# Filling TensorE's planned waits with products of ones, and planning the order for the full clock

## The chip, the cores and the metric

The kernel runs on one core of a Trainium2 chip. The metric is the device time of one execution in microseconds, lower is better. The core has five engines with a queue of their own each, which run in order and wait for one another by semaphores: TensorE (PE in the profile; its weight loads are PEld), VectorE (DVE), ScalarE (ACT), GpSimd (POOL) and SyncE (SP), which issues the transfers here.

## The reference

Two things follow one another. The first is attention with a mask: each query and each key of a head is assigned to the nearest of 16 centroids, and a query sees only the keys of its own cluster. The second is a feed-forward layer over the 3072 rows of the result.

```python
q_assign = np.argmax(np.einsum('bhsd,hcd->bhsc', q_n, c_n), axis=-1)
k_assign = np.argmax(np.einsum('bhsd,hcd->bhsc', k_n, c_n), axis=-1)
mask = q_assign[:, :, :, None] == k_assign[:, :, None, :]
scores = np.where(mask, scale * np.matmul(q, k.transpose(0, 1, 3, 2)), -1e9)
attn = softmax(scores)                    # 4 batches, 8 heads, 768 x 768, head size 64
x = np.matmul(attn, v)                    # as 3072 x 512
h = x @ w_in                              # 512 x 2048
g = np.where(h >= 1, h, np.where(h <= -1, 0.0, (h + 1) ** 2 / 4))
out = g @ w_out                           # 2048 x 512
```

## The kernel before

**The work.** Float32 operands are split into a high and a low float16 part, and each product is made of three products of parts. A pair of heads fills the 128 partitions, so there are 4 pairs in each of 4 batches. The queries are taken in chunks of 256 rows: 3 chunks a batch, 12 in all. For each chunk and head pair there are four score steps (`at_scores`, `at_soft`): products of queries and keys and of the cluster masks into a PSUM bank, a scaling with the row minimum on VectorE (the custom instruction that writes `sS`), the exponential on ScalarE, a split into high and low (`hl`) on ScalarE and GpSimd, and a transpose into `pT`, by the DMA engines or, in the early steps, by TensorE for every other step (the products `idf,sS`). Then `at_av` multiplies the transposed weights by the values into `bank_a`; ScalarE copies one part of it (`rb`) and VectorE multiplies the other by it. The result `x` of four head pairs is one input chunk of the feed-forward part (`ffn1`, `ffn2`).

**The start.** Ahead of the first scores the head pairs' k, q and v are loaded, scaled (`kv_scale`, with a small product of ones that spreads a maximum over the partitions, `am`), split and transposed (products `idf,n`), and assigned to centroids (products `cT,kvq`, then a series of small VectorE instructions). The feed-forward weights are loaded in 16 pieces and prepared during the first part of the run: absolute values on ScalarE, bit operations on VectorE (`wk`, `w`), column sums as products with ones (`wk,ones`), a scale, and a split on ScalarE and GpSimd.

**The order.** Nothing is issued directly. The code records every operation with its engine, its operands and a cost (`price`, in ns); `issue` then plans. `forward` runs the recorded operations through a model of the engines, the PSUM banks and the DMA queue, and takes on each engine the ready operation with the best due time; `backward` computes due times from the end. Eight rounds are made, and the order of the round with the shortest modelled span is issued, each engine in that order. In this model a TensorE operation that starts before `COLD` (75e3 ns) costs twice as much, since TensorE is expected to be at half clock there:

```python
clock[e] = t + x.cost * (2 if e == "tensor" and t < COLD else 1)
```

All instructions are issued from the last lines of `issue` (line 291 in the profile), so lines don't tell them apart there; the tiles' names do. `bank` are the three wide PSUM tiles, `banka` and `bankh` the two single banks. `bank_a` is used by `at_av` alone. `ones` is a 128x128 bfloat16 constant.

Of the kernel before, what the change touches and what calls it, by code (L numbers as in the profile page):

```python
# [27 lines left out]


LATENCY = dict(tensor=280, scalar=252, vector=230, gpsimd=175)  # L30
COLD, AHEAD = 75e3, 1500

LOOK, MARGIN = 0.4, 4000
ROUNDS = 8
# [3 lines left out]
class Recorder:  # L38
# [114 lines left out]
    def forward(self, prio):  # L153

        clock, ready, avail = {}, {}, {}
        left = {x: len(x.preds) for x in self.nodes}
        at = dict.fromkeys(self.nodes, 0.0)
        for x in self.nodes:
            if not x.preds:
                heappush(ready.setdefault(x.eng, []), (0.0, prio[x], x.i))  # L160
        hw, ring, sent, span = 450.0, 0.0, [], 0.0
        self.order, bank = [], {}
        todo = len(self.nodes)
        while todo:
            todo -= 1
            best = None
            for e, q in ready.items():
                now = clock.get(e, 0.0)
                a = avail.setdefault(e, [])
                while q and q[0][0] <= now:  # L170
                    _, s, i = heappop(q)
                    heappush(a, (s, i))
                t = now if a else q[0][0] if q else None
                if t is not None and (best is None or t < best[0]):
                    best = t, e
            t, e = best
            q = ready[e]
            while q and q[0][0] <= t:
                _, s, i = heappop(q)
                heappush(avail[e], (s, i))  # L180
            pick = heappop(avail[e])
            x = self.nodes[pick[1]]

            more = [(s, r, i) for r, s, i in q[:8] if r < t + x.cost * LOOK and s < pick[0] - MARGIN]
            if more:
                heappush(avail[e], pick)
                _, t, i = min(more)
                q.remove((t, prio[self.nodes[i]], i))
                heapify(q)
                x = self.nodes[i]  # L190

            free = max((until for k in x.banks for o, until in bank.get(k, {}).items() if o != e), default=0.0)
            if free > t:
                clock[e] = t
                heappush(q, (free, prio[x], x.i))
                todo += 1
                continue
            if x.dma and x.dma[0] > 256 and ring > t + AHEAD:

                clock[e] = t  # L200
                heappush(q, (ring - AHEAD, prio[x], x.i))
                todo += 1
                continue
            if x.dma:
                kb, tr = x.dma
                t = max(t, hw, sent[-8] if len(sent) > 7 else 0.0)
                clock[e] = t + x.cost
                hw = t + (650 if tr else 475)
                ring = max(ring, hw + (650 if tr else 784)) + kb * (5.6 if tr else 3.25)
                if tr:  # L210

                    hw = max(hw, ring - 1000)
                end = ring + (400 if tr else 1300)
                sent.append(end)
            else:
                clock[e] = t + x.cost * (2 if e == "tensor" and t < COLD else 1)
                end = clock[e] + LATENCY[e]
            for k in x.banks:
                bank.setdefault(k, {})[e] = end
            x.start, x.busy = t, clock[e]  # L220
            span = max(span, end)
            self.order.append(x)
            for y in x.succs:
                raw = x.dma or x.eng != y.eng or (y.preds[x] and x.eng != "tensor")
                at[y] = max(at[y], end if raw else x.busy)
                left[y] -= 1
                if not left[y]:
                    heappush(ready.setdefault(y.eng, []), (at[y], prio[y], y.i))
        return span
# [43 lines left out]
                    heappush(ready.setdefault("sync" if p.dma else p.eng, []), (at[p], -prio[p], -p.i))  # L273
        return start

    def issue(self):
        for x in self.nodes:
            for y in x.preds:
                y.succs.append(x)
        prio = {x: x.step for x in self.nodes}  # L280
        best = None
        for _ in range(ROUNDS):
            span = self.forward(prio)
            if best is None or span < best[0]:
                best = span, self.order
            prio = self.backward({x: x.start for x in self.nodes})
        span, self.order = best
        with self.tc.manual_schedule():
            for x in self.order:
                for fn, args, kw in x.calls:  # L290
                    fn(*args, **kw)  # L291

# [57 lines left out]
def tile_clustered_attention_moe(  # L350
# [10 lines left out]
    nc = tc.nc  # L361
# [6 lines left out]
    P = 128  # L368
# [21 lines left out]
    rec = Recorder(tc)  # L390
# [35 lines left out]
    bank = [psum.tile([P, 1024], F32, name=f"bank{i}") for i in range(3)]  # L426
    bank_a, bank_h = [psum.tile([P, 512], F32, name=f"bank{x}") for x in "ah"]
# [3 lines left out]
    start = iter([0, 1] * 2).__next__  # L431
# [28 lines left out]
    ones = const.tile([P, P], BF16, name="ones")  # L460
# [628 lines left out]
    for s in sorted(ev):  # L1089
        rec.step = s  # L1090
        for fn, args in ev[s]:
            fn(*args)
    rec.issue()


# [30 lines left out]
```

## Time and profile before

| | |
|---|---|
| three runs | 919.07, 917.01, 918.56 us (median 918.56) |
| the profiled execution | 917.96 us, its span on the engines 916.2 us |
| mean granted TensorE clock | 0.961 |
| busy, share of the span | PE 89%, PEld 62%, DVE 68%, ACT 72%, POOL 63% |
| TensorE in 0 to 23, 23 to 46, 46 to 69, 69 to 92 us | 5.71, 13.21, 12.37, 14.54 us busy |
| TensorE's waits up to 90 us, by the engine waited for | VectorE's `bank` 15.1 us in 6 waits, ScalarE's `sS` 11.8 in 5, ScalarE's `n` 6.5 in 1, VectorE's `n` 6.0 in 2 |

A row of the timeline has the start in us, the duration of a group in us, the engine, the line, the operation with output and inputs, the number of instructions, and in brackets the idle time ahead of it with the engine that ended it. The granted clock is a share of full speed as the profiler recorded it. A group's row has the busy time in us, the mean duration of one in ns, and the idle time ahead; matmuls overlap, so busy time over count is less than the mean of one.

### The profile page before, as it was taken

The page shows a single profiled execution, that of the slowest core. Times are in us where ns is not written, and L with a number is a line of the kernel's source. Part 1 is how long each engine was busy: PE and PEld are TensorE (multiplying, and loading weights), DVE is VectorE, ACT ScalarE, POOL GpSimd, SP SyncE. Part 2 cuts the span into 40 slices and gives each one's busy share as a digit, 9 for nine tenths or more (in the row PEclk, how much of TensorE's full clock was granted, in tenths as well). Part 3 has the DMA queues.
Part 4 walks back from the last instruction along what each step waited for, and adds up shares of the span by engine and source line. Part 5 has one row for each costly group of instructions (what it writes and reads, how often), then busy time and mean ns, then how long its engine had stood idle before and what let it go on. Part 6 is the DMA issues. An engine that isn't in the chain of part 4 may idle for free.

```text
span 916.2 us, 19559 instructions
## 1 busy us (share of the span) xinstructions
PE 819.7 (89%) x7462; PEld 566.2 (62%) x7462; DVE 621.8 (68%) x1335; ACT 660.5 (72%) x1145; POOL 580.4 (63%) x521
## 2 busy tenths in 40 slices
PE   2556669899998999999998999999998999999998
PEld 2344446556765766776666666666665666667664
DVE  6999987887796665556987665557868555444232
ACT  5778999979767587778676687678766677776232
POOL 1369888986764667766575677656565666666322
PEclk9756779999999999999999999999999999999999
DMA  9989675658998878868899968878998866666100
GB/s 312 238 204 189 133 208 129 152 120 183 185 201 166 161 141 164 156 147 187 166 205 167 176 124 163 157 155 195 178 196 149 149 132 127 111 121 110 30 24 24
DMA packets 403263, 142.82 MB, mean 156 GB/s; under 512 B 380000, under 2 KB 395360, under 8 KB 403168
## 3 DMA queue, kind: packets, MB, share of 16 engines
q1 hardware_dynamic: 403168, 141.56, 76.3%
q8 instruction: 58, 0.95, 0.4%
q14 instruction: 37, 0.30, 0.1%
HBM read 40.40 MB, written 6.29 MB: 51 GB/s over the span
## 4 chain that ended last, share of the span: by engine, by line
PE 68%; DVE 14%; issue 4%; ACT 2%; POOL 2%; ACTq 0%; DVEq 0%; POOLq 0%
PE bank L291 51%; PE banka L291 10%; PE bankh L291 8%; DVE sS L291 3%; DVE r L291 2%; DVE bank L291 2%; DVE kvq L291 2%; DVE n L291 1%; POOL hl L291 1%; DVE w L291 1%; ACT sS L291 1%; DVE mx L291 1%; ACT hl L291 0%; ACT wk L291 0%; DVE bankh L291 0%
## 5 line engine op out<-in xcount | busy, mean ns | idle before, releaser
L291 POOL TENSOR_TENSOR hl<-sS,hl 128x768 f16<-128x768 f32 x181 | 311.4, 1723 | 138.2 <-ACT hl L291 122.1
L291 PE MATMUL bank<-w,g 128*128 128x512 f16 x1152 | 272.7, 380 | 3.0 <-ACT o L291 1.8
L291 PEld LDWEIGHTS <-w 128*128 128x128 f16 x2304 | 223.8, 98 | 62.4 <-issue 21.7
L291 DVE CUSTOM_DVE_ANT_0 sS<-bank,zero,er 128x768 f32<-128x768 f32 x192 | 194.2, 1012 | 88.6 <-PE bank L291 68.2
L291 PEld LDWEIGHTS <-kvq 128*128 128x128 f16 (+1 forms) x3264 | 191.3, 107 | 88.8 <-issue 43.2
L291 ACT ACTIVATE sS<-sS,sbi 128x768 f32<-128x768 f32 x192 | 179.3, 934 | 87.0 <-DVE sbi L291 83.3
L291 PEld LDWEIGHTS <-g 128*128 128x128 f16 x1152 | 111.1, 98 | 120.6 <-POOL g L291 3.3
L291 PE MATMUL bank<-kvq 128*128 128x384 f16 x768 | 163.1, 337 | 17.4 <-DVE sbi L291 7.7
L291 POOL TENSOR_TENSOR g<-r,g 128x512 f16<-128x512 f32 x88 | 104.5, 1187 | 87.3 <-ACT g L291 87.2
L291 ACT CAST hl<-sS 128x768 f16<-128x768 f32 x181 | 148.8, 825 | 3.1 <-DMA pT<-hl 1.7
L291 PE MATMUL bank<-x,w 128*128 128x256 f16 x1056 | 127.9, 274 | 7.2 <-DVE bank L291 3.5
L291 ACT ACTIVATE r<-r,f_ra,f_rs 128x512 f32<-128x512 f32 x88 | 71.3, 810 | 59.0 <-DVE r L291 58.6
L291 PE MATMUL banka<-pT,kvq 128*64 128x256 f16 x1728 | 105.9, 278 | 0.0
L291 DVE TENSOR_SCALAR r<-bank,f_lo,f_hi 128x512 f32<-128x512 f32 x60 | 48.5, 808 | 39.6 <-PE bank L291 32.7
L291 ACT CAST g<-r 128x512 f16<-128x512 f32 x88 | 53.8, 611 | 22.4 <-DVE r L291 13.9
L291 PE MATMUL bank<-wk,w 128*128 128x256 f16 x504 | 60.2, 273 | 4.0 <-DVE bank L291 1.9
L291 POOL TENSOR_TENSOR w<-w 128x1024 f32<-128x1024 f32 (+1 forms) x24 | 52.1, 2177 | 10.6 <-ACT w L291 10.6
L291 PE MATMUL bankh<-x,w 128*128 128x256 f16 x480 | 57.0, 273 | 1.6 <-DVE r L291 1.5
L291 DVE SCALAR_TENSOR_TENSOR r<-bank,f_gs,r 128x512 f32<-128x512 f32 x60 | 44.8, 746 | 13.3 <-ACT r L291 11.3
L291 POOL TENSOR_TENSOR n<-n,phi 128x768 f16<-128x768 f16 x14 | 21.6, 1540 | 28.9 <-DMA kvq<-n 14.9
L291 ACT ACTIVATION_READ_ACCUMULATOR sS<-sS,sbi 128x1 f32 x192 | 36.0, 187 | 0.0
L291 DVE TENSOR_SCALAR r<-bankh,f_lo,f_hi 128x512 f32<-128x512 f32 x28 | 22.6, 809 | 19.5 <-PE bankh L291 16.7
(180 smaller groups left out, 884.0 us busy)
## 6 DMA issues: line engine op xcount, KB each, us to landing
w<-in_moe_w_out_dram SPq DMA_DIRECT2D x14, 512.0 KB, 4.4
kvq<-in_k_dram SPq DMA_DIRECT2D x16, 384.0 KB, 3.8
kvq<-in_q_dram SPq DMA_DIRECT2D x16, 384.0 KB, 3.9
kvq<-in_v_dram SPq DMA_DIRECT2D x16, 384.0 KB, 4.2
out_dram<-o SPq DMA_DIRECT2D x11, 512.0 KB, 3.8
w<-in_moe_w_in_dram SPq DMA_DIRECT2D x10, 512.0 KB, 5.3
n<-in_moe_w_in_dram SPq DMA_DIRECT2D x6, 512.0 KB, 4.2
o<-in_v_dram SPq DMA_DIRECT2D x8, 384.0 KB, 3.9
```

Source lines behind the costliest of these rows:

```text
L291: fn(*args, **kw)
```

## The change

Two things change, and both act through the order.

`COLD` goes from 75e3 to 15e3: the model doubles TensorE's costs only up to 15 us. The eight rounds are made again with that, so the whole order of all five engines is a new one, with the same operations.

While issuing, the planned start and end of every operation is now known. Ahead of each TensorE operation that is planned to start before 300 us (`WARM`), and that starts over 600 ns (`PAUSE`) after the end of the one before it, products are put in: each multiplies the constant `ones` by four repetitions of itself (512 columns) into `bank_a`, at 217 ns (`FILL`) of the planned wait each, as many as fit, from a planned 10 us on. Nobody reads them. None is put in while a result in `bank_a` is planned to be still unread, and not before the last reader's planned end and latency.

```diff
-COLD, AHEAD = 75e3, 1500
+COLD, AHEAD = 15e3, 1500
+
+
+WARM, PAUSE, FILL = (10e3, 300e3), 600, 217
...
-            self.order.append(x)
+            self.order.append((x, t, x.busy))
...
-    def issue(self):
+    def issue(self, idle, bank):
...
-            for x in self.order:
+            done, free, unread = 0.0, 0.0, set()
+            for x, start, busy in self.order:
+                own = any(name == bank for name, _ in x.banks)
+                if x.eng == "tensor":
+                    t = max(done, free, WARM[0])
+                    while not unread and start < WARM[1] and t + FILL < start and start - done > PAUSE:
+                        idle()
+                        t += FILL
+                    done = busy
+                    if own:
+                        unread = {y for y in x.succs if y.eng != "tensor" and any(name == bank for name, _ in y.banks)}
+                elif own:
+                    unread.discard(x)
+                    free = max(free, busy + LATENCY[x.eng])
                 for fn, args, kw in x.calls:
                     fn(*args, **kw)
...
-    rec.issue()
+    still = ones.unsqueeze(1).to_broadcast([P, 4, P])
+    rec.issue(lambda: nc.tensor.matmul(bank_a, ones, still, start=True, stop=True), bank_a.tensor.name)
```

In the new kernel the products of ones have line 1111, everything else that the planner issues has line 308. The order holds 194 products of ones, each with a weight load. Three places follow.

TensorE at about 17 us, between the maximum of the values (`v_am`) and the scale of the third head pair (`am_132`), before:

```order
L291 MATMUL bank_76<-v_am_130,ones 128x4
L291 LDWEIGHTS ones
L291 MATMUL bank_76<-am_133,ones 128x2
L291 LDWEIGHTS ones
L291 MATMUL bank_75<-wk_66,ones 128x128
...
L291 MATMUL bank_76<-am_132,ones 128x2
L291 LDWEIGHTS n_72
L291 MATMUL bank_74<-idf,n_72 128x128
```

The same place now:

```order
L308 MATMUL bank_76<-v_am_130,ones 128x4
L1111 LDWEIGHTS ones
L1111 MATMUL banka<-ones 128x512
...
L308 MATMUL bank_76<-am_133,ones 128x2
L1111 LDWEIGHTS ones
...
L1111 MATMUL banka<-ones 128x512
L308 LDWEIGHTS ones
L308 MATMUL bank_76<-am_132,ones 128x2
L308 LDWEIGHTS ones
L308 MATMUL bankh<-n_72,ones 128x32
```

Two products of ones stand ahead of `am_133` and sixteen ahead of `am_132`; the eight column sums of the first weights (`wk_66`) have moved to a later place, and the mask sums (`bankh<-n_72,ones`) stand ahead of the transposes (`idf,n_72`).

TensorE at about 60 us, ahead of the third of the transposes of softmax weights (`idf,sS_81`), before:

```order
L291 MATMUL bank_75<-kvq_62 128x384
L291 LDWEIGHTS kvq_62
L291 MATMUL bank_75<-kvq_62 128x384
L291 MATMUL bank_74<-idf,sS_81 128x128 x6
```

The same place now:

```order
L308 MATMUL bank_75<-kvq_62 128x384
L308 LDWEIGHTS kvq_62
L308 MATMUL bank_75<-kvq_62 128x384
L1111 LDWEIGHTS ones
L1111 MATMUL banka<-ones 128x512
...
L1111 MATMUL banka<-ones 128x512
L308 MATMUL bank_74<-idf,sS_81 128x128 x6
```

Twenty-two products of ones stand between the scores (`kvq_62`) and these transposes.

VectorE from the first score step on (`sS` with its minimum `sbi`), before:

```order
L291 ISA sS_80,sbi_156<-bank_74,zero,er_148 128x768
L291 ISA sbi_156 128x1
L291 TENSOR_SCALAR bank_76<-bank_76 128x2
L291 TENSOR_SCALAR wk_66<-wk_66 128x1024
L291 TENSOR_SCALAR bank_76<-bank_76 128x1
L291 ISA sS_81,sbi_157<-bank_75,zero,er_148 128x768
```

The same place now, with the third and second score steps far behind the first:

```order
L308 TENSOR_SCALAR wk_66<-wk_66 128x1024
L308 TENSOR_REDUCE mx_146<-bank_76 128x24
L308 ISA sS_80,sbi_156<-bank_74,zero,er_148 128x768
L308 ISA sbi_156 128x1
L308 TENSOR_SCALAR w_iw_0_119<-bank_75 128x1
...
L308 ISA sS_79,sbi_158<-bank_74,zero,er_148 128x768
...
L308 SCALAR_TENSOR_TENSOR w_73<-w_73,wk_66 128x1024
...
L308 ISA sS_81,sbi_157<-bank_75,zero,er_148 128x768
```

The second score step (`sbi_157`) followed the first after three other instructions; now it stands behind the third (`sbi_158`), and a step of the weights' bit operations (`wk_66`, `w_73`) has moved ahead of each. Across all engines the planned operations are the same as before; the run of ones on TensorE is what is added.

## The prediction

> **What bounds the kernel now.** I read the page first, then the stretches (busy time by engine), then who waits for whom, and last TensorE's instructions in order of time.
>
> ```profile
> span 916.2 us, 19559 instructions
> PE 819.7 (89%) x7462; PEld 566.2 (62%) x7462; DVE 621.8 (68%) x1335; ACT 660.5 (72%) x1145; POOL 580.4 (63%) x521
> 10.00:35.00 25.00, 12.37 (x148) 9.67 (x149) 22.63 (x50) 16.45 (x25) 4.92 (x5) 1.00 0.98 313
> 35.00:92.00 57.00, 33.30 (x333) 24.62 (x332) 55.94 (x108) 44.96 (x59) 42.03 (x27) 0.58 0.92 199
> 92.00:138.00 46.00, 29.00 (x230) 19.97 (x229) 40.53 (x94) 44.11 (x68) 39.70 (x30) 0.78 0.66 169
> 138.00:184.00 46.00, 40.30 (x367) 28.12 (x365) 36.27 (x106) 43.00 (x72) 41.20 (x33) 0.96 0.62 141
> 184.00:916.00 732.00, 704.60 (x6394) 483.67 (x6391) 463.15 (x965) 505.98 (x912) 450.63 (x405) 1.00 0.76 146
> ```
>
> In a stretch's row the columns are its length, then busy us (with instructions) of PE, PEld, DVE, ACT, POOL, then granted clock, DMA share and GB/s. From 184 us on TensorE works 704.60 of 732 us at the full clock: there it is the bound. Before that another engine is full in each stretch: VectorE (55.94 of 57 us up to 92), then ScalarE (44.11 of 46 and 43.00 of 46). TensorE is idle in two fifths of 35 to 138 us, and its clock is 0.58 and 0.78. So a faster TensorE helps in the first part only where the full engine waits for it.
>
> The clock row needs a correction. It says 1.00 up to 35 us, but the same work takes there as long as in the half-clock part:
>
> ```profile
> 28.55 2.72 PE L291 MATMUL bank<-kvq 128*128 128x384 f16 x8 [1.54 <-ACT kvq L291]
> 91.48 1.46 PE L291 MATMUL bank<-kvq 128*128 128x384 f16 x8 [0.30 <-DVE pT L291]
> 19.77 1.01 PE L291 MATMUL bank<-wk,ones 128*128 128x128 bf16 x8 [0.43 <-DVE wk L291]
> 92.78 0.62 PE L291 MATMUL bank<-wk,ones 128*128 128x128 bf16 x8
> ```
>
> Eight score products take 2.72 us at 28.55 and 1.46 at 91.48, eight weight-sum products 1.01 and 0.62. The ratio is 1.86 and 1.63; so TensorE is slow from its first product on.
>
> **The products of ones.** The order holds 194 of them, in 26 runs: 156 ahead of the first attention-times-values group, 28 in four runs up to the first hidden layer's products, and 10 far back in TensorE's full part. The nearest row for one is the other 128x512 product:
>
> ```profile
> L291 PE MATMUL bank<-w,g 128*128 128x512 f16 x1152 | 272.7, 380 | 3.0 <-ACT o L291 1.8
> 17.16 0.17 PE L291 MATMUL bank<-v_am,ones 128*128 128x4 bf16 x1
> 23.33 0.19 PE L291 MATMUL bank<-am,ones 128*128 128x2 bf16 x1 [2.55 <-DVE bank L291]
> 61.81 1.54 PE L291 MATMUL bank<-idf,sS 128*128 128x128 f32 x6 [5.77 <-ACT sS L291]
> ```
>
> That is 272.7 / 1152 = 0.237 us each, and by the ratio 1.86 about 0.44 us at half clock. All 194 are 46 us at the full clock. From 10 to 138 us TensorE is idle 25 + 57 + 46 - 12.37 - 33.30 - 29.00 = 53.3 us now. A mean clock of 0.58 means half clock for 0.84 of the time, 0.78 for 0.44; a full clock would leave 33.30 x 0.42 + 29.00 x 0.22 = 20 us more idle. So they fit in total; they cost nothing where the wait behind them is really there. The run of 22 ahead of the transposes of sS is 22 x 0.237 = 5.2 us in a wait that is 5.77 us now: covered by ScalarE's exponential. The 16 + 2 between v_am and the second am are the worst case, since the clock is still low there: 18 x 0.44 = 7.9 us, in a gap of 23.33 - 17.16 = 6.2 us. The product behind them can be 1.7 us late, and less if the clock rises under way. What covers this is VectorE's queue, full for 22.63 of 25 us: 0 to +1.7 us; I take 0, since 24 transposes stand behind it and gain from the same clock.
>
> **What the faster clock gives.** Who waits for TensorE up to 92 us, and the pieces of the chain that ended last that are TensorE's from 100 to 126 us:
>
> ```profile
> DVE w_am L291 <- PE bank L291: 0.5, 1, 0.5
> DVE kvq L291 <- PE bank L291: 0.4, 1, 0.4
> DVE sS L291 <- PE bank L291: 0.4, 1, 0.4
> DVE sc L291 <- PE bank L291: 0.3, 1, 0.3
> DVE bank L291 <- PE bank L291: 0.2, 1, 0.2
> ...
> 103.16 3.68 PE bank L291 x18
> 106.83 2.31 PE banka L291 x44
> 109.14 0.77 PE bank L291 x4
> 119.54 1.54 PE bank L291 x6
> 121.08 3.66 PE banka L291 x35
> ```
>
> (a) 23 to 92 us. VectorE, the full engine, waits 0.5 + 0.4 + 0.4 + 0.3 + 0.2 = 1.8 us for TensorE. Half the time of the work waited for is the slow clock: -0.9 us. VectorE's own next instruction is late next.
>
> (b) 92 to 138 us. The same groups stand in the timeline slow and fast:
>
> ```profile
> 103.16 1.54 PE L291 MATMUL bank<-idf,sS 128*128 128x128 f32 x6 [3.26 <-ACT sS L291]
> 104.49 1.06 PE L291 MATMUL bank<-wk,ones 128*128 128x128 bf16 x8
> 105.35 1.49 PE L291 MATMUL bank<-kvq 128*128 128x384 f16 x4
> 107.01 2.13 PE L291 MATMUL banka<-pT,kvq 128*64 128x256 f16 x36
> 112.19 0.87 PE L291 MATMUL bank<-idf,sS 128*128 128x128 f32 x6 [1.19 <-ACT sS L291]
> 121.44 3.30 PE L291 MATMUL banka<-pT,kvq 128*64 128x256 f16 x36
> 129.11 0.81 PE L291 MATMUL bank<-kvq 128*128 128x384 f16 x4
> ```
>
> Transposes 1.54 against 0.87, twice; weight sums 1.06 against 0.62; scores 1.49 against 0.81; attention times values 3.30 against 2.13: 1.34 + 0.44 + 0.68 + 1.17 = 3.6 us on the chain. ScalarE is late next: its idle time in the stretch is 46 - 44.11 = 1.9 us, so -1.9 is all it can give.
>
> How far the clock holds here is open. From the run ahead of the first attention-times-values group to the one ahead of the third, over 206 products of the kernel's own, the new order has no product of ones.
>
> ```profile
> 90.00:93.00 3.00, 2.70 (x34) 2.00 (x31) 3.00 (x6) 2.97 (x4) 3.00 (x2) 1.00 1.32 142
> 93.00:96.00 3.00, 1.27 (x13) 0.92 (x11) 2.97 (x14) 2.60 (x6) 3.00 (x2) 1.00 0.97 163
> 96.00:99.00 3.00, 2.53 (x14) 1.51 (x14) 2.69 (x6) 3.00 (x6) 1.91 (x4) 0.59 0.92 337
> 94.81 0.87 PE L291 MATMUL bank<-idf,sS 128*128 128x128 f32 x6 [1.42 <-ACT sS L291]
> ```
>
> At 93 to 96 us TensorE works 1.27 of 3 us, its longest wait is 1.42 us, and right after it the clock is 0.59. So waits of that length let it fall, and I count (b) at the capped -1.9, not at 3.6. The Trainium skill ("TensorE: Matmul & The Clock Gate", section "Why this matters for your kernels") says that gaps between bursts may last up to about 3 us before the clock goes back; this trace disagrees, with 1.42 us as the longest wait ahead of the fall. By that rule the clock would stay up through the unfilled stretch; this is a rival below.
>
> (c) 138 to 184 us. The clock is 0.96, so half-clock time is 0.04 x 46 / 0.5 = 3.7 us; TensorE is busy 88% and loses 3.7 x 0.5 x 0.88 = 1.6 us. The order has 23 products of ones just ahead of this stretch and none in it, so I take a third: -0.5 us.
>
> (d) The new order itself. VectorE and ScalarE hold the same instructions; the last weight instruction of either stands behind the same 36 and 37 score steps as before. Some early weight steps stand ahead of scores that they followed. Nothing prices this: 0, with bounds from the idle time of the full engines from 10 us on, (25 - 22.63) + (57 - 55.94) + 1.9 + (46 - 43.00) = 8.3 us as the most that a better order and clock together can gain, and the rival below as the loss.
>
> **Sum.** -0.9 - 1.9 - 0.5 = -3.3 us on the profiled execution's 917.96, 914.7. That execution is 0.6 us under the median of 918.56; on the median the forecast is 915.3 us. About 0.2% (1.8 us) is what a measurement of this kernel can tell from no change.
>
> **Rivals.**
>
> No change, 918.6 us. The products run, but VectorE and ScalarE set the pace, and their waits for others take the place of the 1.8 and 1.9 us. For it: the full one of the two is above 95% busy from 35 to 138 us. Against it: the chain does pass through TensorE for 12 us there. The same time comes out if the products run at half clock and never lift it. Chance 0.22.
>
> Slower, 922.7 us. TensorE takes its queue in order, so where the wait is shorter than the order's own costs assume, the real product stands behind products of ones. The five longest runs are 16, 14, 18, 17 and 22, 87 products, 20.6 us; if their waits are a fifth shorter than planned, 4.1 us reach VectorE, which is full there. It decides once VectorE's waits for TensorE from 23 to 92 us grow from 1.8 to over 6 us. For it: the runs fill the whole expected wait without a margin, and the first run is planned at half its price. Against it: the 5.77 us wait above holds its run. The Trainium skill (same page, section "Part 2: What happens when you issue a matmul") says that matmuls stay in program order, which would make each late product late in full. Chance 0.25.
>
> The clock holds throughout, 913.3 us. Then (b) gives its 3.6 us, if the new order takes from ScalarE's queue what now stands ahead of those steps, and (c) half of its 1.6: 918.56 - 0.9 - 3.6 - 0.8 = 913.3. The Trainium skill's rule on gaps, above, would have it so. Against it stands the fall after 1.42 us. Chance 0.11.
>
> **The numbers.** The forecast has 0.42. Faster by over 0.2% is the forecast and the last rival, 0.53; within it 0.22; slower 0.25. The range goes up to the slower rival, 922.7, and down to the gain of 8.3 us with 1.8 us for a luckier order in the full part (27.4 us idle from 184 on): 908.5. Cases of both signs matter, so the forecast's own range: 912.5 to 916.7.
>
> **What would show it.** Right: a clock of 0.9 or more from 25 to 80 us, score groups of eight near 1.5 us, VectorE's waits for TensorE under 1 us up to 92, TensorE 95% busy from about 180 us on. Wrong: the clock still near 0.5 in 35 to 92; or real products that start later behind products of ones than their operands; or a gain or loss that arises behind 184 us, which would be the order's and not the clock's.

## The result, and the profile after

The change made the kernel slower: 928.97 us (median of 5 runs, 926.85 to 930.18) against 918.56 us (917.01 to 919.15), a ratio of 1.0114 with a 95% interval of 1.0095 to 1.0133. The forecast was 915.3 us, and its range ended at 922.7.

The profiled execution of the changed kernel took 928.97 us. Its page, to be laid beside the one in the prediction:

```profile
span 927.2 us, 19941 instructions
PE 856.3 (92%) x7656; PEld 578.0 (62%) x7656; DVE 623.8 (67%) x1335; ACT 659.9 (71%) x1145; POOL 573.0 (62%) x521
```

Its stretches (length, then busy us of PE, PEld, DVE, ACT, POOL, then granted clock, DMA share, GB/s):

```profile
10.00:35.00 25.00, 22.85 (x226) 13.69 (x227) 21.06 (x46) 14.78 (x23) 4.70 (x5) 0.93 0.96 309
35.00:92.00 57.00, 46.20 (x386) 27.15 (x384) 55.72 (x116) 47.11 (x64) 40.37 (x25) 0.88 0.89 216
92.00:138.00 46.00, 31.56 (x250) 20.83 (x249) 39.03 (x90) 39.52 (x60) 37.97 (x30) 0.80 0.62 146
138.00:184.00 46.00, 40.86 (x346) 28.11 (x345) 37.01 (x93) 42.19 (x69) 38.75 (x30) 0.98 0.52 121
184.00:916.00 732.00, 706.31 (x6419) 484.90 (x6419) 466.01 (x977) 506.77 (x917) 447.31 (x409) 1.00 0.77 147
```

The products of ones did what they are for: from 35 to 92 us the clock is 0.88 instead of 0.58. VectorE is as full there as before (55.72 of 57 us). From 92 to 138 us the clock gained only 0.02, and ScalarE, which was full with 44.11 us, now works 39.52: taken as a whole, nobody is full in this stretch any more (VectorE still is from 92 to 104 us, with 12.00 of 12 us), and the engines wait for one another.

What TensorE does at the place of its longest new wait, in order of time (start, duration, idle time ahead in brackets):

```profile
100.66 1.46 PE L308 MATMUL bank<-kvq 128*128 128x384 f16 x8 [1.55 <-DVE pT L308]
107.16 1.01 PE L308 MATMUL bank<-wk,ones 128*128 128x128 bf16 x8 [5.04 <-DVE sbi L308]
...
128.88 2.13 PE L308 MATMUL banka<-pT,kvq 128*64 128x256 f16 x36
```

And VectorE there:

```profile
97.08 2.66 DVE L308 SCALAR_TENSOR_TENSOR n<-n,wk 128x1024 uint32<-128x1024 uint32 x1
102.34 2.76 DVE L308 SCALAR_TENSOR_TENSOR w<-w,wk 128x1024 uint32<-128x1024 uint32 x1
105.02 1.00 DVE L308 CUSTOM_DVE_ANT_0 sS<-bank,zero,er 128x768 f32<-128x768 f32 x1
106.11 0.98 DVE L308 CUSTOM_DVE_ANT_0 sS<-bank,zero,er 128x768 f32<-128x768 f32 x1
```

TensorE has the scores done at 102.1 us and then stands still for 5.04 us: its next product needs the bank that a score step reads. On VectorE one of the weights' bit operations, of 2.66 us, has just ended then (97.08); another one, of 2.76 us, stands ahead of that score step (102.34), and two score steps of 1.0 us each run before the bank is free. This wait was made by the order, not by the products of ones: it is there without them too, as the first experiment shows.

From 184 to 525 us, in the part where TensorE is the bound, two groups of its waits for VectorE (us, times, longest) and the stretch, before (two fences) and now (two more):

```profile
PE bank L291 <- DVE bank L291: 2.8, 5, 1.2
PE bank L291 <- DVE sbi L291: 1.8, 3, 0.9
```

```profile
184.00:525.00 341.00, 326.12 (x3065) 224.32 (x3063) 245.45 (x530) 249.39 (x453) 224.35 (x199) 1.00 0.87 168
```

```profile
PE bank L308 <- DVE sbi L308: 6.8, 9, 1.6
...
PE bank L308 <- DVE bank L308: 5.1, 4, 3.0
```

```profile
184.00:525.00 341.00, 322.16 (x3026) 220.90 (x3027) 243.29 (x532) 244.82 (x446) 218.12 (x199) 0.99 0.87 165
```

The waits for a bank that a score step reads (`sbi`) went from 1.8 to 6.8 us. TensorE works 4.0 us less in the same 341 us, and 2.4 us of what it does work are the last ten products of ones (at 0.237 us).

Where the time went can be followed by the attention-times-values groups of 36 products, 48 in all, counted in order of time. The first of them, and VectorE's second score step of the order before (`sbi_157`), before (first two lines) and now:

```profile
34.45 1.00 DVE L291 CUSTOM_DVE_ANT_0 sS<-bank,zero,er 128x768 f32<-128x768 f32 x1
65.88 3.76 PE L291 MATMUL banka<-pT,kvq 128*64 128x256 f16 x36
47.53 1.01 DVE L308 CUSTOM_DVE_ANT_0 sS<-bank,zero,er 128x768 f32<-128x768 f32 x1
72.45 2.13 PE L308 MATMUL banka<-pT,kvq 128*64 128x256 f16 x36
```

The loss arises in two places. The first group already starts 6.6 us late, so most of the early loss is there before the 5.04 us wait; the fourth starts 7.4 us late (121.44 us before, 128.88 now, the last row of TensorE's above). The score step that was moved behind the weight steps runs 13 us later, but no run separates which of the moves makes the first group late. Most of that is caught up: the 14th group is 1.3 us late (315.88 and 317.20). Then the time is lost again, far behind the part that the change is about: the 26th group is 9.6 us late (515.43 and 525.06), and the last one 11.0 us (856.86 and 867.88).

### The profile page after: what moved, and what is told of

Read it like the earlier page. It is cut to its first block, busy times and chain, and to the rows that moved or that the text cites. A ratio compares the mean times of both kernels' runs of the same rounds, so it can differ in the third digit from the quotient of the medians.

```text
span 927.2 us, 19941 instructions
## 1 busy us (share of the span) xinstructions
PE 856.3 (92%) x7656; PEld 578.0 (62%) x7656; DVE 623.8 (67%) x1335; ACT 659.9 (71%) x1145; POOL 573.0 (62%) x521
## 4 chain that ended last, share of the span: by engine, by line
PE 65%; DVE 11%; issue 3%; ACT 3%; POOL 1%; ACTq 0%; DVEq 0%; POOLq 0%
PE bank L308 49%; PE banka L308 8%; PE bankh L308 8%; DVE r L308 2%; DVE sS L308 2%; DVE bank L308 2%; DVE kvq L308 1%; DVE n L308 1%; ACT sS L308 1%; POOL g L308 1%; DVE mx L308 1%; ACT n L308 1%; ACT hl L308 0%; ACT g L308 0%; POOL hl L308 0%
## 5 line engine op out<-in xcount | busy, mean ns | idle before, releaser
L308 POOL TENSOR_TENSOR hl<-sS,hl 128x768 f16<-128x768 f32 x181 | 306.1, 1695 | 137.1 <-ACT hl L308 120.4
L308 PEld LDWEIGHTS <-kvq 128*128 128x128 f16 (+1 forms) x3264 | 187.9, 105 | 86.4 <-issue 41.5
L308 PE MATMUL bank<-kvq 128*128 128x384 f16 x768 | 158.7, 330 | 18.9 <-DVE sbi L308 10.3
L1111 PE MATMUL banka<-ones 128*128 128x512 bf16 x194 | 52.3, 417 | 2.7 <-DVE rb L308 2.7
L1111 PEld LDWEIGHTS <-ones 128*128 128x128 bf16 x194 | 19.6, 106 | 30.8 <-issue 16.0
```

The source lines that it names most:

```text
L1111: rec.issue(lambda: nc.tensor.matmul(bank_a, ones, still, start=True, stop=True), bank_a.tensor.name)
```

## The experiments

Two theories stood at the start. O: the new order costs the time. F: the products of ones cost it, by standing ahead of real products. Ratios are to runs of the kernel before on the same chip (918.0 to 918.4 us).

**The order alone.** The changed kernel without any product of ones; the order of everything else is the same.

```diff
-WARM, PAUSE, FILL = (10e3, 300e3), 600, 217
+WARM, PAUSE, FILL = (10e3, 0.0), 600, 217
```

> The new order (planned with COLD at 15e3) without any product of ones; the kernel's own work is unchanged. Theory O, the order costs the time: the loss of 10.4 us stays, 926 to 931 us, and TensorE's own work is some 9 to 12 us behind before's at 525 us, with most of that lost between 250 and 525 us. Theory F, the products of ones cost it by standing ahead of real products: 917 to 920 us without them. Theory B, both by about half: 922 to 925 us.

Measured: 932.08 us, ratio 1.0151 (1.0133 to 1.0170). Its stretches (first fence) and TensorE's wait at the same place as above (second):

```profile
35.00:92.00 57.00, 30.96 (x275) 21.92 (x273) 52.77 (x112) 44.20 (x58) 36.76 (x23) 0.59 0.85 209
184.00:525.00 341.00, 319.25 (x2982) 217.51 (x2980) 245.01 (x537) 245.66 (x450) 216.98 (x196) 0.98 0.86 163
```

```profile
110.95 1.01 PE L308 MATMUL bank<-wk,ones 128*128 128x128 bf16 x8 [5.03 <-DVE sbi L308]
```

Theory O holds, 1 us above its range, and F falls: without products of ones it is even slower, by 3.1 us, the 5.03 us wait is there, and from 184 to 525 us TensorE works 319.25 us against 326.12 before, 6.9 us less. So the new order costs 13.7 us, and the products of ones give 3.4 us back on it (1.0151 to 1.0114 of 918 us).

What they give back can be seen in VectorE's waits for TensorE from 23 to 92 us, the view from which the prediction took its 1.8 us on the order before. Here are the two largest without products of ones (6.5 us in all) and the only one with them:

```profile
DVE bank L308 <- PE bank L308: 3.0, 3, 1.0
DVE w_am L308 <- PE bank L308: 2.3, 1, 2.3
```

```profile
DVE bank L308 <- PE bank L308: 1.9, 2, 1.7
```

On an order that was planned for the full clock, the full engine waits 6.5 us for a TensorE at half clock, and a faster one has something to give. On the order before there were 1.8 us.

**The products of ones alone.** Before's order with products of ones in its planned waits.

```diff
-COLD, AHEAD = 15e3, 1500
+COLD, AHEAD = 75e3, 1500
```

> Before's order, word for word, with products of ones in its planned waits (168 of them, since the plan with COLD at 75e3 has other waits). Theory O: within 2 us of before, 917 to 921 us; before's order gains nothing from the clock, since VectorE and then ScalarE are full, and loses nothing. Theory F: 925 to 930 us. A variant of my prediction, the faster clock alone helps: 914 to 917 us.

Measured: 919.15 us, ratio 1.0005 (0.9995 to 1.0014): no difference. Its stretches (first fence), and TensorE at the chain's place from 115 us on (second):

```profile
35.00:92.00 57.00, 42.00 (x377) 26.15 (x377) 55.42 (x109) 44.01 (x58) 40.85 (x27) 0.76 0.85 195
92.00:138.00 46.00, 34.98 (x276) 22.04 (x276) 40.19 (x94) 44.07 (x69) 39.39 (x29) 0.93 0.67 173
```

```profile
115.82 2.72 PE L308 MATMUL bank<-kvq 128*128 128x384 f16 x8 [2.83 <-DVE sbi L308]
118.34 2.96 PE L1111 MATMUL banka<-ones 128*128 128x512 bf16 x12
121.13 0.82 PE L308 MATMUL bank<-idf,sS 128*128 128x128 f32 x6
122.13 2.13 PE L308 MATMUL banka<-pT,kvq 128*64 128x256 f16 x36
```

This is the cleanest answer on the clock. The clock is 0.76 for 0.58 and 0.93 for 0.78, the transposes take 0.82 us for 1.54 and the attention-times-values group 2.13 for 3.30, all as the prediction had it, and the kernel is not faster. VectorE works 55.42 of 57 us and ScalarE 44.07 of 46, as before. The faster group starts later: the transposes ran at 119.54 before and at 121.13 now. Only 0.3 us of that is the twelve products of ones ahead of them, since the exponential whose result they transpose ends at 120.8. The rest is the clock again: behind a wait of 2.83 us in which no product of ones stands, the eight scores at 115.82 take 2.72 us (1.74 before), and VectorE's score step behind them starts at 118.69 instead of 117.39.

**Another order, planned for less of the half clock.** Before with one number changed, no products of ones.

```diff
-COLD, AHEAD = 75e3, 1500
+COLD, AHEAD = 60e3, 1500
```

> Before with COLD at 60e3 instead of 75e3 and no product of ones: another order made by the same planner. If orders of this planner scatter by some 10 us whatever their model is, this one lies more than 4 us from 918.6, to either side. If the loss comes from planning for a clock that isn't there (the model too fast), this one lies between, 919 to 923 us. If orders differ little, 917 to 920 us.

Measured: 924.63 us, 1.0072 (1.0050 to 1.0094). It is 6 us off and above the 919 to 923 of the theory that a too fast model costs by degrees. The scatter of orders became a theory of its own, S.

**Products of ones only up to 100 us.**

```diff
-WARM, PAUSE, FILL = (10e3, 300e3), 600, 217
+WARM, PAUSE, FILL = (10e3, 100e3), 600, 217
```

> The changed kernel with products of ones only ahead of products planned before 100 us: 156 instead of 194. Theory O: 927 to 931 us, as the changed kernel. Theory F with the cost in the later 38 (those between 100 and 300 us, where TensorE's work falls behind): 919 to 923 us. If the later ones help by holding the clock: 931 to 935 us.

Measured: 927.78 us, 1.0110 (1.0088 to 1.0132), the same as the changed kernel. The 38 later products neither cost nor give anything that can be measured; the 3.4 us come from the first 156.

**Half of each order.** The planner is run for both values of `COLD`; the operations that the first plan starts before 200 us are issued in its order, the rest in the other's. No products of ones.

```diff
+SPLIT = 200e3
...
+        first, then = self.plan(15e3), self.plan(75e3)
+        head = [o for o in first if o[1] < SPLIT]
+        taken = {o[0] for o in head}
+        self.order = head + [o for o in then if o[0] not in taken]
```

> No products of ones. The new order for every operation planned to start before 200 us, before's order for the rest, in which TensorE is the bound. In the traces the new order without products of ones loses some 5 us up to 184 us and 11.6 us of TensorE time between 184 and 525 us. Theory L, the later loss is in the later order itself: this one loses only the early part, 921 to 925 us. Theory E, the early order leaves the engines in a state from which the later loss follows whatever the order there: 928 to 933 us.

Measured: 922.23 us, 1.0047 (1.0035 to 1.0060). And with the two plans exchanged:

> No products of ones. Before's order for every operation planned to start before 200 us, the new order for the rest. Theory L: 925 to 930 us, with TensorE waiting for VectorE's score steps at 290 to 350 and 445 to 500 us as in the changed kernel. Theory E: 917 to 921 us.

Measured: 924.18 us, 1.0068 (1.0049 to 1.0088). TensorE from 184 to 525 us, with the new order early (its wait for score steps, then the stretch) and late (the same two):

```profile
PE bank L317 <- DVE sbi L317: 2.1, 4, 0.9
```

```profile
184.00:525.00 341.00, 325.85 (x3088) 224.62 (x3086) 247.03 (x544) 249.44 (x459) 223.86 (x201) 1.00 0.90 170
```

```profile
PE bank L317 <- DVE sbi L317: 8.1, 8, 1.6
```

```profile
184.00:525.00 341.00, 319.73 (x3023) 220.18 (x3023) 241.91 (x522) 244.81 (x441) 219.77 (x196) 1.00 0.87 166
```

The later loss belongs to the later order: with before's order from 200 us on TensorE works 325.85 us there and waits 2.1 us for score steps, with the new one 319.73 and 8.1, although its first 200 us are before's. Theory L holds (the second run lies 0.8 us under its range, 3 us above E's). Both halves cost, 4.1 us the early and 6.1 us the late one; together 10.2 of the 13.7 us. Whether the other 3.5 us are an effect of both together is not shown. The three intervals leave room for most of it, and 2.9 us of it are there where the two kernels still issue the same instructions in the same order: the eighth attention-times-values group starts at 203.74 us in the profile of the order alone and at 200.80 in that of its early half.

**Does it matter what the order was planned for?** One number of the model that has nothing to do with the clock, how far transfers may be queued ahead, was moved by 3%, with `COLD` as before and as changed. No products of ones.

```diff
-COLD, AHEAD = 75e3, 1500
+COLD, AHEAD = 75e3, 1450
```

> Before with one number of the planner's model that has nothing to do with TensorE's clock moved a little (how far transfers may be queued ahead, 1450 ns for 1500); COLD stays 75e3. Theory S, the planner's orders scatter by some us with any touch and before's is a lucky one: off by more than 3 us, 922 to 932 us. Theory M, it is planning for a clock that is too fast that costs: 916.5 to 920.5 us.

Measured: 925.63 us, 1.0079 (1.0065 to 1.0093).

```diff
-COLD, AHEAD = 75e3, 1500
+COLD, AHEAD = 15e3, 1450
```

> The same small move of that number, with COLD at 15e3 and no products of ones. Theory M: 929 to 935 us, as the new order without products of ones at 932.1. Theory S: more than 3 us away from 932.1, to either side, most likely better, 920 to 929 us.

Measured: 926.33 us, 1.0102 (1.0082 to 1.0123). Theory M falls and S holds: a touch that leaves the clock alone costs 7.5 us, and the same touch on the order planned for the full clock brings it down by 5.8 us (4.5 by the ratios). Part of the loss stands in TensorE's full part again; here is the first of the two from 184 to 525 us, the waits and the stretch:

```profile
PE bank L291 <- DVE r L291: 7.5, 7, 2.5
PE bank L291 <- DVE bank L291: 5.9, 5, 2.8
PE bank L291 <- DVE sbi L291: 5.5, 7, 1.2
```

```profile
184.00:525.00 341.00, 318.18 (x2993) 219.59 (x2990) 242.85 (x524) 244.23 (x441) 217.56 (x195) 0.99 0.87 163
```

It works 8 us less than before's 326.12 there, waiting for VectorE; the second one works 321.41 us, 4.7 us less.

**A model nearer to the clock that is there.** The trace of before shows the half clock again and again up to 137 us, and once more at 175 us.

```diff
-COLD, AHEAD = 75e3, 1500
+COLD, AHEAD = 130e3, 1500
```

> Before with COLD at 130e3, near the 137 us up to which the trace of before shows the half clock again and again; no products of ones. If the order is the better, the truer the model's clock: 910 to 917 us. Theory S, orders scatter and before's is a lucky one: 921 to 932 us.

Measured: 931.64 us, 1.0137 (1.0117 to 1.0157). The truer model gave a bad order, which is S again. Six orders of this planner are now timed without products of ones: 918.6, 924.6, 925.6, 926.3, 931.6 and 932.1 us. Before's is the fastest of them, by 6 us. Whether its two numbers, 75e3 and 1500, had been chosen among several by their time is not on record; if they had, its neighbours would be slower for that reason alone.

**Is the clock worth something when no product is late for it?** Before's order, products of ones in the first half of each planned wait only.

```diff
-                    while not unread and start < WARM[1] and t + FILL < start and start - done > PAUSE:
+                    while not unread and start < WARM[1] and t + FILL < (done + start) / 2 and start - done > PAUSE:
```

> Before's order with products of ones in only the first half of each planned wait (75 of them instead of 168), so that a real product is seldom behind one. Theory Q, the clock is worth some us and the queue of products of ones takes them back: 915 to 917 us here. Theory N, VectorE and ScalarE are full and the clock is worth nothing on this order: 917.5 to 919.5 us, with VectorE's score steps in the first 90 us less late than the 0.8 us that all 168 cost.

Measured: 917.42 us, 0.9994 (0.9985 to 1.0002). Its stretch (first fence), and VectorE's waits for TensorE from 23 to 92 us (us, times, longest), the two largest here (second) and with all 168 products of ones (third):

```profile
35.00:92.00 57.00, 36.57 (x356) 24.14 (x356) 55.99 (x110) 45.51 (x60) 42.10 (x28) 0.73 0.91 198
```

```profile
DVE kvq L308 <- PE bank L308: 0.5, 1, 0.5
DVE sS L308 <- PE bank L308: 0.4, 1, 0.4
...
```

```profile
DVE bank L308 <- PE bank L308: 1.5, 2, 1.3
DVE sS L308 <- PE bank L308: 0.9, 1, 0.9
...
```

The time lies between the ranges of the two theories, 0.1 us from N's. The clock is 0.73, the waits for TensorE are 1.3 us for 1.8 before and 2.6 with all products, and the time differs from before's by less than the interval. That interval leaves room for a gain of up to 1.4 us, so N is the better fit and Q's smallest gain is not excluded. The two terms that the prediction weighed up to 92 us were a gain of 0.9 us and late products of 1.7 us at most. The waits fell by 0.5 us here, the longest wait with all products is 1.3 us, and neither can be seen in the time. On the stretch from 92 to 138 us this run says little, since its clock there is 0.81, hardly above before's 0.78.

**Products of ones on the two other orders.** The kernels with the transfer number at 1450, with products of ones up to 300 us.

```diff
-COLD, AHEAD = 15e3, 1500
+COLD, AHEAD = 15e3, 1450
```

> The other order planned for the full clock (COLD at 15e3, the transfer number at 1450; 926.3 us without products of ones) with products of ones in all its planned waits up to 300 us, 213. Theory P, an order that was planned for the full clock gets back some us when the clock is really there, as the changed kernel got 3.1: 921 to 924.5 us. Theory N: 925.5 to 928 us.

Measured: 925.44 us, 1.0080 (1.0066 to 1.0095), against 1.0102 (1.0082 to 1.0123) without.

```diff
-COLD, AHEAD = 15e3, 1500
+COLD, AHEAD = 75e3, 1450
```

> The other order planned for half clock up to 75 us (COLD at 75e3, the transfer number at 1450; 925.6 us without) with products of ones in its planned waits, 154. Theory P: nothing, 924.5 to 927 us, as on before's order. If products of ones help any order but before's: 921 to 924 us.

Measured: 926.54 us, 1.0096 (1.0082 to 1.0111), against 1.0079 (1.0065 to 1.0093) without. The direction is that of theory P, some gain on an order planned for the full clock and none on one planned for half clock, but the intervals of both pairs overlap and the first stayed outside P's 921 to 924.5 us. P is not shown by the times. The traces support it. Here are VectorE's waits for TensorE from 23 to 92 us in the profiled executions, without and with products of ones, beside what the products did to the time (each from its two ratios; in the first two rows it is the one ratio to before):

| order | waits without, us | waits with, us | change of the time, us |
|---|---|---|---|
| before's, all products | 1.8 | 2.6 | +0.5 |
| before's, first half of each wait | 1.8 | 1.3 | -0.6 |
| the changed kernel's (`COLD` 15e3) | 6.5 | 1.9 | -3.4 |
| `COLD` 15e3, transfers 1450 | 5.5 | 3.0 | -2.0 |
| `COLD` 75e3, transfers 1450 | 0.8 | 1.4 | +1.6 |

Of the changes of the time only the -3.4 us is clear of the intervals. But all five have the sign of the change of the waits, and the two largest gains stand where VectorE waited longest. Orders differ by more than any of this.

No run was faster than before beyond its interval, so there is no better version to offer.

## Why the prediction was wrong

**The step that failed is (d), the new order itself.** The prediction put it as: "Nothing prices this: 0, with bounds from the idle time of the full engines ... and the rival below as the loss." The order alone measured +13.7 us. The rival that stood for the loss, 4.1 us, was about late products, so the order had no bound of its own on that side. The mistake in it can be named: the bound was taken from idle time that could be gained (8.3 us up to 184 us, and 1.8 us behind it), as if an order could only fill waits. A re-made order can also open new waits, and everywhere: 6.1 us came from its part behind 200 us, to which the prediction gave a small possible gain and no possible loss. That VectorE and ScalarE "hold the same instructions" was true and said nothing, since who stands ahead of whom decides the waits: TensorE's waits for score steps from 184 to 525 us went from 1.8 to 6.8 us. Why an order of this planner comes out better or worse by some us stays open.

**(a), (b) and (c), the clock.** The sizes of the single pieces came out: the transposes at 0.82 us, the attention-times-values group at 2.13. The sum of -3.3 us was measured as +0.5 us (-0.5 to +1.3 by the interval) on before's order, where it was worked out. (a) and (b) each had a step wrong. In (b), ScalarE's idle time of 1.9 us from 92 to 138 us was taken as what the faster chain would fill. But ScalarE did not wait for TensorE there. Its waits in that stretch, before (first two lines) and with products of ones on the same order:

```profile
ACT sS L291 <- DVE sbi L291: 1.3, 4, 0.5
ACT wk L291 <- issue: 0.4, 1, 0.4
ACT sS L308 <- DVE sbi L308: 1.3, 2, 1.1
```

They are waits for VectorE's score steps, and they are as long with the faster clock; ScalarE's 44.11 us became 44.07. VectorE's own waits for TensorE there grew, from 1.5 to 2.5 us, the longest of them at 118.69 behind the scores at half clock. In (a), the waits were read off the order before, while the kernel runs the new one, where they are 6.5 us without products of ones. So on the new order the products of ones gave 3.4 us, near the sum, but at other waits; that nearness is luck.

**The price of the products.** The group from 10 to 300 us, 188 of the 194, and one piece of it in order of time:

```profile
L1111 PE MATMUL banka<-ones 128*128 128x512 bf16 x188 | 49.9, 413 | 2.7 <-DVE rb L308 2.7
```

```profile
135.58 0.81 PE L1111 MATMUL banka<-ones 128*128 128x512 bf16 x3 [2.70 <-DVE rb L308]
```

49.9 / 188 is 0.265 us each, over both clocks; the forecast was 0.237 at the full and 0.44 at half clock. Once, at 135.58 us, a product of ones waited itself, 2.70 us, for VectorE to read `bank_a`, with the transposes behind it in TensorE's queue; the prediction had no term for that. It cost nothing here, since the exponential that the transposes need ended at 136.4 us and they started at 136.44.

**The rivals.** "Slower" had the right sign for the wrong reason: its condition, VectorE's waits for TensorE from 23 to 92 us over 6 us, was not met (1.9 us in the changed kernel). "No change" is what the products of ones gave by themselves. "The clock holds throughout" did not happen, as the fall after 1.42 us had warned: the clock is 0.80 from 92 to 138 us.

**What was announced as proof.** The stretch that the prediction named, in the changed kernel:

```profile
25.00:80.00 55.00, 48.93 (x442) 27.67 (x439) 52.18 (x116) 41.72 (x56) 31.37 (x21) 0.99 0.86 212
```

The clock of 0.9 from 25 to 80 us came (0.99), and so did a TensorE that is 95% busy from 184 us on (706.31 of 732 us). VectorE's waits for TensorE under 1 us did not come (1.9 us). And "a gain or loss that arises behind 184 us, which would be the order's and not the clock's", named there as a sign of being wrong, came as a loss. The sign was there; the forecast gave it no price.

## What to carry to other kernels

When a change makes a planner or a scheduler plan anew, price the new order as a risk of its own before any effect that the change is about: here a 3% touch of an unrelated number cost 7.5 us, twice the whole effect under study, and five other orders all lost 6 to 14 us to the one that was there. To see what a change is worth, hold the order fixed and change only the rest; the two experiments that did so separated the two effects at once. And read what a faster clock may give from the waits of the full engine for the faster one, on the order that will run: here 1.8 us on the order before, where it gave nothing that can be measured although single pieces nearly halved, and 6.5 us on the new one, where it gave 3.4 us.

## What the runs showed of the hardware that was not expected

A short stretch of waiting is enough to bring the clock down even in the part where TensorE is full. In the changed kernel it waits 2.96 us at 443 us, and right behind that its clock is half for a while (the wait and the products behind it in order of time, then the two stretches around its end):

```profile
446.04 0.18 PE L308 MATMUL bank<-am,ones 128*128 128x2 bf16 x1 [2.96 <-DVE bank L308]
446.73 4.44 PE L308 MATMUL bank<-w,g 128*128 128x512 f16 x12
```

```profile
440.00:447.00 7.00, 4.04 (x23) 1.84 (x21) 6.55 (x10) 4.01 (x8) 3.27 (x4) 1.00 0.94 228
447.00:451.00 4.00, 4.00 (x12) 1.46 (x11) 2.73 (x11) 2.76 (x5) 2.33 (x4) 0.57 0.54 99
```

The twelve products take 4.44 us there and 2.75 us at the full clock (at 440.33 us), so the wait of 2.96 us costs 1.7 us more. The length of one wait does not decide it alone. Before's order has one wait of 1.48 us at 291 us, with TensorE busy on both sides, and its clock stays at 1.00. In the run with the new order late, waits of 0.45, 0.63 and 0.98 us stand close together from 708 to 711 us, with TensorE busy 1.33 of 3 us, and the clock is 0.57 in the 3 us behind. So the prediction's reading, that waits of 1.42 us let the clock fall, was too simple: there too TensorE was busy only 1.27 of 3 us.
